# Sixteen more ticks behind the gate columns, the high parts of q on GpSimd, and fewer maxima taken off by VectorE, in a kernel of attention and two expert layers

## The chip, the cores and the metric

One core of one Trainium2 chip. The metric is the device time of one execution in microseconds (us), the median of three runs. Names: PE is TensorE, DVE is VectorE, ACT is ScalarE, POOL is GpSimd, and SP (SyncE) issues most of the loads.

## The reference, cut to what matters

Attention with random features, then a product of four weights, then an expert layer in which each token goes to one expert. Inputs are float32; the weights of the middle part come to the chip as float64 words and are turned into float32 there.

```python
def phi(x):                                   # x is q or k, 2 x 8 heads x 576 tokens x 64
    proj = np.einsum('bhsd,md->bhsm', x, omega)          # 128 features
    h = proj - np.sum(x * x, axis=-1, keepdims=True) / 2.0
    h = h - np.max(h, axis=-1, keepdims=True)
    return np.exp(h) / np.sqrt(m)
q_p, k_p = phi(q_s), phi(k_s)
kv, z = np.einsum('bhsm,bhsd->bhmd', k_p, v), np.sum(k_p, axis=2)
x = np.einsum('bhsm,bhmd->bhsd', q_p, kv) / (np.einsum('bhsm,bhm->bhs', q_p, z)[..., None] + 1e-06)
x = ((x @ w1) * (x @ w2)) @ w3 @ w_out        # 1152 tokens, 512 -> 1024 -> 1024 -> 512
...
expert_idx = np.argmax(x @ w_gate, axis=1)    # 8 experts, capacity 288 tokens
h = np.maximum(np.einsum('ecd,edf->ecf', disp, e1), 0.0)
y = np.einsum('ecf,efd->ecd', h, e2)          # weighted by the gate, scattered back to the tokens
```

## The kernel before, in words

Every large matrix product is done with operands split into a high part (rounded to a TensorE format) and a low part (what rounding left): three matmuls, high by high, low by high, high by low. So each operand needs a copy that rounds and a subtraction, on whichever engine is chosen for it, before PE may use it.

**Attention** (to about 100 us). Tokens come in nine tiles of 128, first of k (k0 to k8), then of q (q0 to q8). `split` (L195) makes the high part with an ACT copy (L198) and the low part with a subtraction on POOL (L199; DVE for k0 and k2). `phi` (L202) does a group of four heads: twelve matmuls (L210), a maximum on DVE (L212), and then one of two ways. With the group in `SUBK` or `SUBQ`, DVE subtracts the maximum (L215) and ACT does one exponential of 512 columns (L216); otherwise ACT does four exponentials of 128 columns with the maximum as bias (L219). `q_tr` (L221) transposes the features of q, which ACT copies out (L227); `num` (L254) and `x_tr` (L272) make x and its two parts.

**Weights.** A chunk of 128x512 float64 words goes through five steps: a load (SP), three bit operations on DVE (L325 to L327, or L350, L351 and L355), a cast to the high part on ACT (L330 or L360), the low part on POOL (L331 or L364). The float32 words `w_f` have two buffers, which the low part on POOL sets free.

**Middle** (to about 250 us). PLAN gives the order of PE's work: `ab` (L425) are the products x@w1 and x@w2 of one block f of 128 columns, whose product g is made by DVE (L448) or, for some, by ACT and POOL (L445, L446); `W` (L465) is w3@w_out of one block, copied out twice by ACT (L478, L479) and its low part made by POOL (L480); `gate_t` (L487) and `gate_u` (L496) make the columns of W times w_gate, with the ACT copies L494 and L501; `logits` use these.

**Order.** PE's order is that of the text throughout. Up to the mark "|" in PLAN a scheduler places the instructions of DVE, ACT, POOL and SP; behind it those engines too keep the order of the text, and each works strictly in its order. Behind the mark, conversions of weights are tasks in a list; `tick()` (L133) hands out the next stage of up to two tasks that hold a raw buffer, one stage per engine and tick. Ticks stand behind each half of `ab`, inside and behind `W` and behind `logits`. `need` ticks until a weight is there.

**Experts** (from about 230 us). END is the order of the last stretch, a letter per step and "." for a tick. `r0` and `r1` are the first expert chunk of each batch half. For each: `to_features` (letters t, T; L812) transposes gathered rows, with ACT L824 and DVE L825; `product` (p, P; L830) multiplies by W, with copies L839 (ACT) and L840 (DVE); `hidden` (h, H; L845) multiplies by e1 and `result_t` (s, S; L885) by e2, with ACT L898, transposes L901, and `scatter` (L868): DVE L870 and an indirect DMA by POOL to `out` (L871). The expert weights have no float64 step: load by SP (L739), high parts of their two halves on ACT (L752), low part of half 0 on DVE and of half 1 on POOL (L756); the low part of half 1 sets the raw buffer free for the next load. The quarters 0 and 2 share one ring of two raw buffers, 1 and 3 another of two. A digit in END lets the tasks of a matrix start: "3" is e1 of r1, "4" is e2 of r1; "x" and "y" hand these tasks in. In the names of the trace the numbers of experts and buffers are left out: `r_e_20h` is the high part of half 0 of quarter 2, of e1 or e2, of either chunk.

Of the kernel before, what the change touches and what calls it, by code (L numbers as in the profile page):

```python
# [33 lines left out]
DVE_LOW = ("k0", "k2")  # L34

SUBK = [(0, 1), (), (0, 1), (0, 1), (), (), (), (), ()]
SUBQ = [(1,), (0, 1), (0, 1), (1,), (), (1,), (1,), (), (1,)]

KV_AT = {2: (0,), 4: (1, 2), 6: (3, 4), 8: (5, 6), 10: (7, 8)}

# [14 lines left out]

END = "l<kAkrArfAAArfw>AAAA>AA<At.ttLttMt>1K.p..K.p..Rp..p..p..RpF.2h..h.R.h..Fh..h..h..x3h..h..s.TT.sTT.sTT.s..ssy4P..P..P..P..P..P..P.H.H.H.H.H.HHHSSSS"


@with_exitstack
def attention_moe_kernel(ctx: ExitStack, tc: tile.TileContext, qT, kT, v, om, w1, w2, w3, wo, wg, e1, e2, cap, out):
    nc = tc.nc
    V = nc.vector
    A = nc.scalar
# [15 lines left out]
    def px(nm):  # L81
        return psx.tile([128, 512], F32, tag="px", name=nm)
# [4 lines left out]
    def kq(shape, dt, nm):  # L87
        return kqp.tile(shape, dt, tag="kq", name=nm)

    def wt(tag, shape, dt, nm):  # L90
        return big.tile(shape, dt, tag=tag, name=nm, bufs=BUFS[tag])
# [20 lines left out]
    late, hold, leave = [False], [False], set()  # L112
# [9 lines left out]
    def pump():  # L122
        full = set()
        for t in todo:
            r = t["ring"]
            if r and t["raw"] is None and r not in full:
                if out_of[r] < LIM[r]:
                    out_of[r] += 1
                    t["raw"] = t["load"]()
                else:  # L130
                    full.add(r)

    def tick(n=1):  # L133
        for _ in range(0 if hold[0] else n):
            used = set()
            while todo and (todo[0]["key"][0][0] != "e" or todo[0]["key"][:2] in leave) and (todo[0]["ring"] is None or sum(t["ring"] is not None for t in active) < 2):
                active.append(todo.pop(0))
            for t in list(active):
                engs, fn, end = t["st"][0]
                if used & set(engs):  # L140
                    continue
                used |= set(engs)
                t["st"].pop(0)
                fn(t)
                if end:
                    out_of[t["ring"]] -= 1
                    pump()
                if not t["st"]:
                    active.remove(t)
                    done_of[t["key"]] = t["got"].get("r", True)  # L150
# [44 lines left out]
    def split(src, i, nm):  # L195
        t = wt("hl", [128, 2, 512], F32R, f"{nm}{i}_hl")
        raw = src[i].rearrange("p k t -> p (k t)")
        A.copy(out=t[:, 0], in_=raw)  # L198
        (V if nm + str(i) in DVE_LOW else nc.gpsimd).tensor_tensor(out=t[:, 1], in0=raw, in1=t[:, 0].bitcast(F32), op=ALU.subtract)  # L199
        return t  # L200

    def phi(dst, t, g, nm, sub):  # L202

        ps = pa(f"pj{nm}_{g}")
        p3 = ps.rearrange("p (h m) -> p h m", m=M)
        mx = sm.tile([128, 4], F32, tag="mx", name="mx", bufs=4)
        for r in range(2):
            k = 2 * g + r
            for n, (s, w) in enumerate(PASS):
                nc.tensor.matmul(out=ps[:, r * 256:(r + 1) * 256], lhsT=t[:, s, k * 128:(k + 1) * 128], rhs=om_hl[:, w],  # L210
                                 start=(n == 0), stop=(n == 2))
        V.tensor_reduce(out=mx, in_=p3, axis=AX, op=ALU.max, negate=True)  # L212
        d3 = dst[:, 4 * g:4 * g + 4, :]
        if g in sub:
            V.tensor_tensor(out=d3, in0=p3, in1=mx.unsqueeze(2).to_broadcast([128, 4, M]), op=ALU.add)  # L215
            A.activation(out=d3, in_=d3, func=ACTF.Exp)  # L216
        else:
            for h in range(4):
                A.activation(out=d3[:, h, :], in_=p3[:, h, :], func=ACTF.Exp, bias=mx[:, h:h + 1])  # L219
# [83 lines left out]
    def split_to(n):  # L303
        while len(hls) < min(n, 18):
            w, i = order[len(hls)]
            load_to(len(hls) + 1 + AHEAD)
            hls[len(hls)] = split(kt if w == "k" else qt, i, w)

    def phi_g(n, g):
# [3 lines left out]
        if g == 0:  # L313
            split_to(n + 1)
            (kp if w == "k" else qp)[i] = wt("ph", [128, H, M], F32, f"{w}p{i}")
        phi((kp if w == "k" else qp)[i], hls[n], g, f"{w}{i}", (SUBK if w == "k" else SUBQ)[i])

# [169 lines left out]
    def gate_t(f):  # L487

        raw = raws.pop(f)
        ps = px(f"wT{f}")  # L490
        for d in range(4):
            nc.tensor.transpose(out=ps[:, d * 128:(d + 1) * 128], in_=raw[:, d * 128:(d + 1) * 128], identity=ident)
        wT[f] = kq([128, 4, 128], F32, f"wT{f}")
        A.copy(out=wT[f], in_=ps.rearrange("p (d m) -> p d m", d=4))  # L494

    def gate_u(f):  # L496
        ps = px(f"u{f}")
        t = wT.pop(f)
        for d in range(4):
            nc.tensor.matmul(out=ps[:, 0:E], lhsT=t[:, d], rhs=wgT[:, d], start=(d == 0), stop=(d == 3))  # L500
        A.copy(out=u_all[:, f], in_=ps[:, 0:E])  # L501

    def logits(f, cs):
        for c in cs:
            nc.tensor.matmul(out=lgp[c * 32:c * 32 + E, 0:C], lhsT=u_all[:, f], rhs=g_t[f][:, c * C:(c + 1) * C],
                             start=(f == 0), stop=(f == 7))
        if late[0]:
            tick()
# [70 lines left out]
    for p in PLAN.split():  # L579
# [10 lines left out]
        elif what == "u":  # L590
            gate_t(*arg)
        elif what == "v":
            gate_u(*arg)
        elif what == "o":
            conv_o(*arg)
        elif what == "t":
            conv3(*arg)
        elif what == "l":
            logits(*arg, range(4))
        elif what == "h":  # L600
            logits(*arg, range(2))
        elif what == "e":
            for w in range(2):
                ab_mm(*arg, w)
        elif what == "z":
            zeroed()
        elif what == "|":
            flush()
            late[0] = True
            mark()  # L610
        elif what == "g":

            wg_sb = kq([E, DM], F32, "wg_sb")
            nc.sync.dma_start(out=wg_sb, in_=wg)
            ps = px("wgT")
            for d in range(4):
                nc.tensor.transpose(out=ps[:, d * E:(d + 1) * E], in_=wg_sb[:, d * 128:(d + 1) * 128], identity=ident[:E, :E])
            A.copy(out=wgT, in_=ps[:, 0:4 * E].rearrange("p (d e) -> p d e", e=E))
# [341 lines left out]

    for p in END:
        if p == "A":
# [119 lines left out]
```

## Time and profile before

| | us |
|---|---|
| three runs | 343.56, 344.31, 346.01 |
| median | 344.31 |
| the profiled execution | 343.41 |
| its span | 341.5 |
| around the span | 1.9 |
| PE busy | 325.2 (95%) |
| DVE busy | 218.8 (64%) |
| ACT busy | 146.4 (43%) |
| POOL busy | 134.2 (39%) |

The span runs from the first to the last instruction that the profile shows. A row of a timeline reads: start, duration, engine, line, operation, what it writes and reads, how many in a row, and in brackets how long the engine had been idle before it and who ended that.

### The profile page before, as it was taken

What the parts mean: (1) busy time and instruction counts of PE and PEld (TensorE: products, weight loads), DVE (VectorE), ACT (ScalarE), POOL (GpSimd) and SP (SyncE); (2) the same over time, 40 slices, a digit from 0 to 9 for tenths busy, and PEclk for the clock granted to TensorE, in tenths of its full rate; (3) what the DMA queues carried; (4) which work ended last, traced back from release to release, by engine and by line L of the source; (5) the groups of instructions that cost most, each with busy time, mean ns of one, the idle gap of its engine ahead of it and who ended that gap; (6) DMA issues with size and microseconds to landing.
All of it is one profiled execution on the core that took longest, in us unless ns stands there. A gap on an engine that the chain in (4) does not pass through costs nothing. (4 is left out here: it accounts for less than half of the span.)

```text
span 341.5 us, 7108 instructions
## 1 busy us (share of the span) xinstructions
PE 325.2 (95%) x2771; PEld 300.8 (88%) x2771; DVE 218.8 (64%) x426; ACT 146.4 (43%) x347; POOL 134.2 (39%) x118
## 2 busy tenths in 40 slices
PE   8999989999999999999998898999999998999991
PEld 6899889999998889898878786899899998999991
DVE  4979999999986864935394763281596766332110
ACT  4999899743321413324333332121462645332100
POOL 3737910333353324545336664014062562243021
PEclk9999999999999999999999999999999999999997
DMA  7995200344465728972335430893869791510011
GB/s 253 396 316 199 64 2 7 97 147 125 126 184 163 270 38 190 211 148 61 125 89 157 134 114 0 289 129 88 298 112 183 224 274 41 209 48 2 1 30 46
DMA packets 25147, 47.76 MB, mean 140 GB/s; under 512 B 3116, under 2 KB 12460, under 8 KB 25110
## 3 DMA queue, kind: packets, MB, share of 16 engines
q1 hardware_dynamic: 16950, 40.18, 39.0%
q10 hardware_dynamic: 7104, 3.54, 6.3%
q0 software_dynamic: 1056, 3.54, 3.8%
q8 instruction: 24, 0.39, 0.5%
q14 instruction: 13, 0.11, 0.1%
HBM read 38.98 MB, written 8.27 MB: 138 GB/s over the span
## 5 line engine op out<-in xcount | busy, mean ns | idle before, releaser
L433 PE MATMUL ab<-xh,w_hl 128*128 128x288 f32 x512 | 108.2, 299 | 4.8 <-POOL w_hl L364 3.8
L433 PEld LDWEIGHTS ab<-xh,w_hl 128*128 128x128 f32 x512 | 83.4, 188 | 8.1 <-POOL w_hl L364 4.5
L433 PE MATMUL ab<-xl,w_hl 128*128 128x288 f32 x256 | 75.5, 295 | 0.0
L433 PEld LDWEIGHTS ab<-xl,w_hl 128*128 128x128 f32 x256 | 48.1, 188 | 0.0
L472 PE MATMUL W<-wo_hl,w_hl 128*128 128x512 f32 x192 | 46.3, 397 | 0.0
L472 PEld LDWEIGHTS W<-wo_hl,w_hl 128*128 128x128 f32 x192 | 35.5, 188 | 8.2 <-issue 0.5
L350 DVE TENSOR_SCALAR w_f<-w_raw 128x512 uint32<-128x512 uint32 x22 | 17.4, 789 | 23.5 <-POOL w_hl L364 23.4
L364 POOL TENSOR_TENSOR w_hl<-w_f,w_hl 128x512 fp32r<-128x512 f32 x22 | 29.6, 1358 | 5.3 <-ACT w_hl L360 5.3
L405 DVE STREAM_TRANSPOSE gs<-g 128x576 f32<-128x576 f32 x16 | 19.5, 1221 | 13.5 <-POOL g L446 13.3
L836 PE MATMUL r_x2p<-r_xc,W 128*128 128x288 f32 x192 | 26.5, 297 | 0.0
L836 PEld LDWEIGHTS r_x2p<-r_xc,W 128*128 128x128 f32 x192 | 25.7, 188 | 0.1
L480 POOL TENSOR_TENSOR W<-W_raw,W 128x512 fp32r<-128x512 f32 x8 | 10.8, 1355 | 37.3 <-ACT W L479 19.2
L331 POOL TENSOR_TENSOR wo_hl<-wo_f,wo_hl 128x512 fp32r<-128x512 f32 x8 | 11.5, 1433 | 34.7 <-PE xT L276 18.4
L437 ACT COPY a_sb<-ab 128x288 f32<-128x288 f32 x32 | 12.7, 398 | 27.6 <-PE ab L433 27.6
L331 POOL TENSOR_TENSOR w_hl<-w_f,w_hl 128x512 fp32r<-128x512 f32 x10 | 14.0, 1402 | 22.4 <-ACT w_hl L330 22.4
L360 ACT CAST w_hl<-w_f 128x512 fp32r<-128x512 f32 x22 | 13.7, 625 | 18.8 <-DVE w_f L355 18.8
L446 POOL TENSOR_TENSOR g<-a_sb,b_sb 128x288 f32<-128x288 f32 x12 | 10.6, 879 | 25.0 <-ACT b_sb L445 25.0
L355 DVE SCALAR_TENSOR_TENSOR w_f<-w_raw,w_f 128x512 uint32<-128x512 uint32 x22 | 19.2, 872 | 0.6
L871 POOL DMA_INDIRECT out<-r_yo,r_odx x6 | 5.6, 932 | 34.4 <-DVE r_yo L870 22.6
L448 DVE TENSOR_TENSOR g<-a_sb,ab 128x288 f32<-128x288 f32 x20 | 8.9, 448 | 15.4 <-PE ab L433 15.4
L210 PE MATMUL pjq<-om_hl,q_hl 128*128 128x256 f32 x108 | 16.3, 293 | 0.0
L210 PE MATMUL pjk<-om_hl,k_hl 128*128 128x256 f32 x108 | 15.6, 297 | 0.6 <-ACT k_hl L198 0.5
(233 smaller groups left out, 693.3 us busy)
## 6 DMA issues: line engine op xcount, KB each, us to landing
w_raw<-in_w SPq DMA_DIRECT2D x32, 512.0 KB, 3.7
wo_raw<-in_wo SPq DMA_DIRECT2D x8, 512.0 KB, 3.5
gd<-gs ACTq DMA_DIRECT2D x12, 288.0 KB, 6.0
v<-in_v SPq DMA_DIRECT2D x9, 260.0 KB
k<-in_kT SPq DMA_DIRECT2D x9, 256.0 KB, 4.3
q<-in_qT SPq DMA_DIRECT2D x9, 256.0 KB, 6.6
out<-zero SPq DMA_DIRECT2D x1, 2304.0 KB, 9.7
r_e_0r<-in_e SPq DMA_DIRECT2D x4, 512.0 KB
```

What stands on the lines that cost most here:

```text
L210: nc.tensor.matmul(out=ps[:, r * 256:(r + 1) * 256], lhsT=t[:, s, k * 128:(k + 1) * 128], rhs=om_hl[:, w], start=(n == 0), stop=(n == 2))
L331: nc.gpsimd.tensor_tensor(out=hl[1], in0=f.bitcast(F32), in1=hl[0].bitcast(F32), op=ALU.subtract)
L350: V.tensor_scalar(out=f, in0=r[:, :, 1], scalar1=3, scalar2=0x3FFFFFF8, op0=ALU.logical_shift_left, op1=ALU.bitwise_and)
L355: V.scalar_tensor_tensor(out=t["f"], in0=r[:, :, 0], scalar=29, in1=t["f"], op0=ALU.logical_shift_right, op1=ALU.bitwise_or)
L360: A.copy(out=h[:, 0], in_=t["f"].bitcast(F32))
L364: nc.gpsimd.tensor_tensor(out=h[1], in0=t["f"].bitcast(F32), in1=h[0].bitcast(F32), op=ALU.subtract)
L405: V.transpose(out=sts[b][:, :, :, f % GF], in_=g_t[f][:, b * S:(b + 1) * S].rearrange("p (j t) -> p j t", t=32))
L433: nc.tensor.matmul(out=p[:, :C], lhsT=w12[f][w][s][:, k, :], rhs=xhl[c][r][:, k], start=(n == 0), stop=(n == 11))
L437: A.copy(out=abp[f, c], in_=p[:, :C])
L472: nc.tensor.matmul(out=p, lhsT=w3_t[f, k // 4][s][:, k % 4, :], rhs=wo_t[k][r], start=(n == 0), stop=(n == 23))
L480: nc.gpsimd.tensor_tensor(out=w_t[f][:, 1], in0=raw, in1=w_t[f][:, 0].bitcast(F32), op=ALU.subtract)
L836: nc.tensor.matmul(out=p4[d][:, :C], lhsT=w_t[f][:, s, d * 128:(d + 1) * 128], rhs=xc[r][f // 4][:, f % 4], start=(f == 0 and (s, r) == (0 ...
```

## The change

Four edits. (1) `SUBQ` keeps four of the nine groups of q whose maximum DVE takes off: q1 group 0, q2 group 0, q5, q6 and q8 group 1 go to the way with four exponentials on ACT. (2) The high part of the nine tiles of q is copied by POOL and no longer by ACT; k stays. (3) `gate_t` and `gate_u` each end with a tick: sixteen in all. (4) In END, "3" moves from right behind "x" to behind the first "TT"; between "3" and "y4" stood ten ticks, and now six.

```diff
-SUBQ = [(1,), (0, 1), (0, 1), (1,), (), (1,), (1,), (), (1,)]
+SUBQ = [(1,), (1,), (1,), (1,), (), (), (), (), ()]
...
-END = "...x3h..h..s.TT.sTT.sTT.s..ssy4P..P.....
+END = "...xh..h..s.TT.3sTT..sTT..s..ssy4P..P.....
...
     def split(src, i, nm):
         t = wt("hl", [128, 2, 512], F32R, f"{nm}{i}_hl")
         raw = src[i].rearrange("p k t -> p (k t)")
-        A.copy(out=t[:, 0], in_=raw)
+        (A.copy if nm == "k" else nc.gpsimd.tensor_copy)(out=t[:, 0], in_=raw)
...
     def gate_t(f):
...
         A.copy(out=wT[f], in_=ps.rearrange("p (d m) -> p d m", d=4))
+        if late[0]:
+            tick()
...
     def gate_u(f):
...
         A.copy(out=u_all[:, f], in_=ps[:, 0:E])
+        if late[0]:
+            tick()
```

Lines from `gate_t` on have numbers two, and from `gate_u` on four higher in the changed kernel.

What moves on POOL in the attention, at the first tiles of q (`w_0_hl` and `w_1_hl` are low parts of w1 and w2, blocks 0 and 1). Before:

```order
L199 TENSOR_TENSOR q_hl<-q_343,q_hl 128x512
L331 TENSOR_TENSOR w_0_hl<-w_0_f,w_0_hl 128x512
L199 TENSOR_TENSOR q_hl<-q_377,q_hl 128x512
L331 TENSOR_TENSOR w_0_hl<-w_0_f,w_0_hl 128x512
L199 TENSOR_TENSOR q_hl<-q_446,q_hl 128x512
L199 TENSOR_TENSOR q_hl<-q_478,q_hl 128x512
L331 TENSOR_TENSOR w_1_hl<-w_1_f,w_1_hl 128x512
```

Of the changed kernel, from the same place:

```order
L198 CAST q_hl<-q_343 128x512
L199 TENSOR_TENSOR q_hl<-q_343,q_hl 128x512
L198 CAST q_hl<-q_377 128x512
L199 TENSOR_TENSOR q_hl<-q_377,q_hl 128x512
L198 CAST q_hl<-q_446 128x512
L199 TENSOR_TENSOR q_hl<-q_446,q_hl 128x512
L198 CAST q_hl<-q_478 128x512
L199 TENSOR_TENSOR q_hl<-q_478,q_hl 128x512
L198 CAST q_hl<-q_580 128x512
L331 TENSOR_TENSOR w_0_hl<-w_0_f,w_0_hl 128x512
```

The first low part of a weight stood behind one row of q and now stands behind nine.

What moves on POOL around block 5 of W (`w_5_hl` are the low parts of w1 and w2 of block 5, in this order; `w_6_0_hl` one of w3; W_2501 and W_2515 are W of block 5). Before:

```order
L364 TENSOR_TENSOR w_5_hl<-w_5_f,w_5_hl 128x512
L480 TENSOR_TENSOR W_2501<-W_raw,W_2501 128x512
L364 TENSOR_TENSOR w_5_hl<-w_5_f,w_5_hl 128x512
L446 TENSOR_TENSOR g_2549<-a_sb,b_sb 128x288
L364 TENSOR_TENSOR w_6_0_hl<-w_6_0_f,w_6_0_hl 128x512
```

Of the changed kernel:

```order
L364 TENSOR_TENSOR w_5_hl<-w_5_f,w_5_hl 128x512 x2
L480 TENSOR_TENSOR W_2515<-W_raw,W_2515 128x512
L364 TENSOR_TENSOR w_6_0_hl<-w_6_0_f,w_6_0_hl 128x512
L446 TENSOR_TENSOR g_2568<-a_sb,b_sb 128x288
```

The low part of w2 passed from behind W's low part to ahead of it; blocks 6 and 7 read alike.

What moves on POOL at the end of r0 (the rows r_e are low parts of e1 of r1, quarters 0 to 3; the one that follows them, again r_e_00l, is of e2 of r1). Before:

```order
L756 TENSOR_TENSOR r_e_00l<-r_e_0r,r_e_00h 128x512
L756 TENSOR_TENSOR r_e_10l<-r_e_1r,r_e_10h 128x512
L756 TENSOR_TENSOR r_e_20l<-r_e_2r,r_e_20h 128x512
L756 TENSOR_TENSOR r_e_30l<-r_e_3r,r_e_30h 128x512
L871 DMA out<-r_yo_3878,r_odx 1152x512
L871 DMA out<-r_yo_3883,r_odx 1152x512
L871 DMA out<-r_yo_3888,r_odx 1152x512
L756 TENSOR_TENSOR r_e_00l<-r_e_0r,r_e_00h 128x512
```

Of the changed kernel:

```order
L760 TENSOR_TENSOR r_e_00l<-r_e_0r,r_e_00h 128x512
L760 TENSOR_TENSOR r_e_10l<-r_e_1r,r_e_10h 128x512
L875 DMA out<-r_yo_3881,r_odx 1152x512
L875 DMA out<-r_yo_3886,r_odx 1152x512
L875 DMA out<-r_yo_3891,r_odx 1152x512
L760 TENSOR_TENSOR r_e_20l<-r_e_2r,r_e_20h 128x512
L760 TENSOR_TENSOR r_e_30l<-r_e_3r,r_e_30h 128x512
L760 TENSOR_TENSOR r_e_00l<-r_e_0r,r_e_00h 128x512
```

The low parts of quarters 2 and 3 of e1 of r1 passed from ahead of the three scatters to behind them. ACT's order at the product of r1 is the same in both: two casts of quarter 2 of e2, the copy L839 of the product's third part, two casts of quarter 3, the fourth copy.

## Rows read from the trace of the kernel before

**Rows 1.** The page's first part: busy time, share, instructions

```profile
PE 325.2 (95%) x2771; PEld 300.8 (88%) x2771; DVE 218.8 (64%) x426; ACT 146.4 (43%) x347; POOL 134.2 (39%) x118
```

**Rows 2.** Windows: stretch, length, busy of PE, PEld, DVE, ACT, POOL; clock, DMA, GB/s

```profile
20.00:40.00 20.00, 19.89 (x328) 18.61 (x330) 18.66 (x29) 18.58 (x56) 12.34 (x9) 1.00 0.49 163
40.00:60.00 20.00, 18.62 (x268) 17.32 (x264) 18.91 (x56) 18.11 (x51) 4.38 (x4) 1.00 0.12 31
```

**Rows 3.** Waits of PE: who, for whom, us in total, times, longest

```profile
PE ab L433 <- POOL w_hl L364: 3.8, 3, 1.5
PE tq L226 <- ACT qpT L227: 1.4, 1, 1.4
...
PE r_pt L820 <- DVE r_xc L825: 0.9, 1, 0.9
```

**Rows 4.** PE's timeline behind W of block 5

```profile
181.74 0.53 PE L433 MATMUL ab<-xh,w_hl 128*128 128x288 f32 x2 [1.02 <-POOL w_hl L364]
```

**Rows 5.** POOL's timeline of the same stretch

```profile
174.20 1.29 POOL L364 TENSOR_TENSOR w_hl<-w_f,w_hl 128x512 fp32r<-128x512 f32 x1 [1.28 <-ACT w_hl L360]
179.17 1.29 POOL L480 TENSOR_TENSOR W<-W_raw,W 128x512 fp32r<-128x512 f32 x1 [3.68 <-ACT u_all L501]
180.42 1.26 POOL L364 TENSOR_TENSOR w_hl<-w_f,w_hl 128x512 fp32r<-128x512 f32 x1
```

**Rows 6.** ACT's timeline of the same stretch

```profile
177.26 0.62 ACT L360 CAST w_hl<-w_f 128x512 fp32r<-128x512 f32 x1 [3.14 <-DVE w_f L355]
```

**Rows 7.** Groups of instructions by form: busy us, mean ns of one, idle before

```profile
L199 POOL TENSOR_TENSOR q_hl<-q,q_hl 128x512 fp32r<-128x512 f32 x9 | 12.7, 1428 | 0.0
...
L219 ACT ACTIVATE qp<-pjq,mx 128x128 f32<-128x128 f32 x36 | 10.4, 409 | 0.0
...
L215 DVE TENSOR_TENSOR qp<-pjq,mx 128x512 f32<-128x512 f32 x9 | 6.1, 685 | 0.0
L198 ACT CAST q_hl<-q 128x512 fp32r<-128x512 f32 x9 | 6.1, 750 | 0.0
L216 ACT ACTIVATE qp<-qp 128x512 f32<-128x512 f32 x9 | 5.7, 645 | 0.2 <-DVE qp L215 0.2
...
L571 POOL MEMSET zero<- 128x512 f32 x1 | 0.5, 518 | 0.0
```

**Rows 8.** DVE's timeline in the attention: the same bit operation twice

```profile
21.66 0.42 DVE L325 TENSOR_SCALAR w_f<-w_raw 128x512 uint32<-128x512 uint32 x1
...
34.82 1.33 DVE L325 TENSOR_SCALAR w_f<-w_raw 128x512 uint32<-128x512 uint32 x1
```

**Rows 9.** POOL's timeline at the scatters of r0

```profile
293.80 0.97 POOL L871 DMA_INDIRECT out<-r_yo,r_odx  x1 [2.29 <-DVE r_yo L870]
300.67 0.95 POOL L871 DMA_INDIRECT out<-r_yo,r_odx  x1 [5.91 <-DVE r_e_20l L756]
304.22 0.92 POOL L871 DMA_INDIRECT out<-r_yo,r_odx  x1 [2.60 <-DVE r_x2l L840]
305.16 1.31 POOL L756 TENSOR_TENSOR r_e_00l<-r_e_0r,r_e_00h 128x512 fp32r<-128x512 f32 x1
```

**Rows 10.** PE's timeline: product of r1, and its hidden layer's first matmul

```profile
292.64 13.02 PE L836 MATMUL r_x2p<-r_xc,W 128*128 128x288 f32 x96
305.51 0.30 PE L857 MATMUL r_hp<-r_x2h,r_e_00h 128*128 128x288 f32 x1
```

**Rows 11.** ACT's timeline: third copy of the product of r1

```profile
303.31 0.40 ACT L839 CAST r_x2h<-r_x2p 128x288 fp32r<-128x288 f32 x1 [0.96 <-PE r_x2p L836]
```

**Rows 12.** SP's timeline: issue of the load of e2's quarter 2

```profile
290.89 0.33 SPq L739 DMA_DIRECT2D r_e_2r<-in_e  x1
```

**Rows 13.** DMA issues: count, KB, median us to landing

```profile
r_e_1r<-in_e SPq DMA_DIRECT2D x4, 512.0 KB, 3.6
```

**Rows 14.** Windows at the end: the clock is the column behind POOL

```profile
334.00:335.00 1.00, 0.54 (x4) 0.18 (x2) 0.42 (x1) 0.00 (x0) 0.00 (x0) 1.00 0.00 0
...
337.00:338.00 1.00, 0.00 (x0) 0.00 (x0) 0.00 (x0) 0.00 (x0) 0.00 (x0) 0.79 0.71 197
```

More of the change, by code (lines that the diff above doesn't have):

```diff
@@ L53 @@
 )
-END = "l<kAkrArfAAArfw>AAAA>AA<At.ttLttMt>1K.p..K.p..Rp..p..p..RpF.2h..h.R.h..Fh..h..h..x3h..h..s.TT.sTT.sTT.s..ssy4P..P..P..P..P..P..P.H.H.H.H.H.HHHSSSS"
+END = "l<kAkrArfAAArfw>AAAA>AA<At.ttLttMt>1K.p..K.p..Rp..p..p..RpF.2h..h.R.h..Fh..h..h..xh..h..s.TT.3sTT..sTT..s..ssy4P..P..P..P..P..P..P.H.H.H.H.H.HHHSSSS"
 @with_exitstack
```

## The prediction

> **What bounds the kernel now.** First the page's first part: PE is busy for 325.2 of 341.5 us, 95% [rows 1], so the kernel is bound by PE wherever nothing makes PE wait, and no edit takes a matmul away. What can be won is what PE waits for, what can be lost is a new wait. So the waits of PE come next [rows 3]: three times, 3.8 us in all, it waits for a weight's low part from POOL; once for 1.4 us, in the attention, for a copy by ACT; once for 0.9 us for the low part of gathered rows near the end. Then, for each of these, the timelines of the engine that is waited for. The windows show who has room in the attention: from 20 to 60 us DVE and ACT are busy for over 18 of each 20 us, POOL for 12.34 of the first 20 and 4.38 of the second [rows 2].
>
> **The added ticks (edit 3).** They issue no new instruction: they hand out stages of conversions sooner. The wait at 181.74 us is that for w2 of block 5 [rows 4]. Its cast was done at 177.26 + 0.62 = 177.88 us [rows 6]. But POOL's next instruction in order was W's low part, which waited for ACT's copies until 179.17, and only behind it, at 180.42, came the low part that PE wanted [rows 5]. It could have run from 177.88 to 179.1, 2.5 us sooner than it ended (180.42 + 1.26 = 181.7). In the new order it stands ahead of W's low part; the other two waits are of the same kind, for blocks 6 and 7, and the longest of the three is 1.5 us [rows 3], all under 2.5. W's low part comes 1.3 us later in exchange, and nothing reads it before the experts, so that costs nothing. What is late next would be the step ahead, the cast and DVE's words; the ticks bring these forward too. Bounds: 0 (another stage is late in its place) and -3.8; I take **-3.8**, since the order removes the very cause that the rows show.
>
> **The attention (edits 1 and 2).** ACT loses nine copies, 6.1 us in all; five groups go from one exponential of 5.7 / 9 = 0.63 us to four of 10.4 / 36 = 0.29 us, which adds 5 x (1.16 - 0.63) = 2.6. ACT: -3.5 us. DVE loses five subtractions of 0.685: -3.4 us. POOL gains nine copies of 128x512 [rows 7]. No row shows such a copy. From below it is bounded by POOL's fill of the same tile, which reads nothing, 0.52 us, from above by its subtraction, which reads two tiles, 1.43 us; it reads one, so I take the middle, 1.0, that is 9.0 us (4.7 to 12.9). POOL has 20 - 12.34 = 7.7 us free from 20 to 40 us [rows 2], where most of these copies fall: 1.3 us too much. What stands behind is the low parts of the first weights (the order shows the first of them behind nine rows of q where it stood behind one). These set the two word buffers free, so DVE, working in order, waits for them with the maxima of q behind: +1.3 at most for PE. The second cost is on DVE: its bit operation takes 0.42 us alone and 1.33 beside POOL's subtractions [rows 8], 0.9 more. POOL has no pauses left, so more of them meet: I count three more, 2.7 us. DVE's relief of 3.4 covers most of it: 1.3 + 2.7 - 3.4 = **+0.6**. PE's wait of 1.4 us hangs on the same chain (ACT's copy behind a cast that waits for DVE's words), so I let it stay. Bounds: copies of 0.52 fit into the gaps, and the 1.4 goes, -1.5 with what ACT gains; copies of 1.43 are 12.9 - 7.7 = 5.2 too many, and with the relief some +4.
>
> The rows show 0.42 against 1.33 us for the same operation [rows 8]. The Trainium skill, "SBUF — State Buffer", section "Who interferes with whom", says that DVE and GpSimd share a pair of ports that one instruction holds to its end while the other stands still. It speaks against this edit, and the row agrees: by it every one of the nine copies could hold up one operation of DVE, the second rival below, where my sum has three. The page "GPSIMD Engine Reference", section 3.1, has 769 ns for 512 elements in a loop with one input; no row here shows it. Nine of these would be an estimated 6.9 us, which fits into POOL's gaps, and the sum would lose its 1.3.
>
> **The end (edit 4).** Fewer casts of expert weights now stand on ACT ahead of the copies of gathered rows, so PE's wait of 0.9 us [rows 3] should go: -0.9. But the low parts of quarters 2 and 3 of e1 of r1 now stand behind POOL's three scatters. Let T be the start of the product of r1 (292.64) [rows 10]. The scatters started at T + 1.2, T + 8.0 and T + 11.6 [rows 9]; the second and third are put down to DVE instructions whose results they don't use, so I read these gaps as the wait until the scatter before has landed, all three writing the same output. In before the load of quarter 2 of e2 was issued at 290.89, ahead of T [rows 12]. Now its buffer comes free only behind a low part that follows the third scatter. The gaps were 6.9 and 3.6 us; three loads ran beside the first, of which two now come later, so I take 4.5 and 3.6: third scatter T + 9.3 to 10.2, the low parts (1.3 each [rows 9]) until 11.5 and 12.8, load issued at 11.6, landed 3.6 later [rows 13] at T + 15.2. ACT's order is unchanged: two casts of that quarter (0.62, as [rows 6], some 1.1 together) come ahead of the third copy of the product (0.40 [rows 11]), whose low part on DVE follows with about as much: ready at T + 17.2. PE ends the product at T + 12.9 [rows 10] and can do 12 more matmuls of 12.87 / 96 = 0.134 us without that part, until T + 14.5: it waits 2.7 us. The fourth part, behind quarter 3's casts, comes 1.3 + 0.3 later, 0.8 of it beyond PE's next six matmuls: 3.5 in all. With -0.9 that is **+2.6**. Bounds: with the gaps as they were (6.9), +5.0; if the scatters don't wait, -0.9.
>
> **Sum.** -3.8 + 0.6 + 2.6 = -0.6 on the profiled execution, which took 343.41 us (span 341.5 and 1.9 around it): 342.8. The median of the runs shown, 344.31, lies 0.9 higher: **343.7 us**. Within 1%, 3.4 us, a measurement of this kernel can hardly tell a change from none; this is within.
>
> **Rivals.**
> First, *the scatters don't wait for each other*. Then POOL issues them at T + 1.2 to 4, the low parts are done by T + 7, the loads land by T + 11, and PE never waits: 343.41 - 3.8 + 0.6 - 0.9 = 339.3, as a median 340.2; with the attention at its better bound 338.1. For it: the rows name DVE and no transfer as what ended the gaps [rows 9]. Against: the gaps are there, 5.91 and 2.60 us, and a scatter uses nothing of what these DVE instructions make.
>
> Second, the other side: *POOL's copies hold DVE in the attention*, all nine and not three. Nine times 0.9 is 8.2 us on DVE; with the 1.3 and less the 3.4 that is +6.1: 343.41 - 3.8 + 6.1 + 2.6 = 348.3, as a median 349.2. It decides from about five operations so held on, where DVE's relief is used up (5 x 0.9 = 4.5 against 3.4), DVE being over 93% busy there [rows 2]. Against: POOL's low parts already run beside DVE for 12 of 20 us, and PE is still 19.89 of 20 busy.
>
> Third, *the ticks move nothing that PE sees*: DVE's words are late instead. 343.41 + 0.6 + 2.6 = 346.6, as a median 347.5. Against: the cast lay ready for 2.5 us.
>
> A further cost is left outside the cases: PE's clock falls after a long pause. At the end it was still at its upper level (1.00, 2.4 GHz) when PE stopped at about 334.5 us and fell to the lower (1.2 GHz) at about 337.6 (0.79 as the mean of that microsecond) [rows 14], 3 us later. [...]
>
> **How the numbers follow.** Forecast 0.48; first rival 0.25; second 0.19; third 0.08. Faster by over 1% (under 340.9) come 0.20 of the first rival and 0.06 of the forecast's lower edge (both terms at their good ends); slower by over 1% (over 347.8) 0.16 of the second, 0.04 of the third and 0.06 of the forecast with the long gap. That is 0.26, 0.48 and 0.26. The range goes from 339.5, within the first rival, to 349.0, within the second; the forecast's own is 341 to 347.5 (tail from +1.7 to +5.0, attention from -1.5 to +2).
>
> **What would show it.** Right: no wait of PE's x products for POOL's low parts; three scatters of r0 in a row with gaps of 3 to 5 us, loads of e2's quarters 2 and 3 issued about 11 us behind the start of r1's product, and PE waiting 2 to 4 us for the third part's low half. In the attention POOL without gaps from 20 to 45 us, the copy at about 1 us, PE's idle time about as before. Wrong: hidden of r1 starting without a wait (first rival); copies over 1.3 us, with PE waiting for maxima or exponentials (second); 3 to 4 us of waits left at blocks 5 to 7 (third).

## The result and the profile after

The changed kernel took 348.05 us in the median of four runs (347.24 to 349.04), the kernel before 344.12: a ratio of 1.0108 with a 95% interval of 1.0076 to 1.0141. It is slower by 1.1%, where the forecast was no change (343.7): inside the whole range (339.5 to 349.0), and above the forecast's own (341 to 347.5). The profiled execution took 347.24 us, 3.8 more than that of before.

The page's first part of the changed kernel, which answers to [rows 1], and its waits of PE, which answer to [rows 3]:

```profile
PE 325.7 (94%) x2771; PEld 300.9 (87%) x2771; DVE 216.8 (63%) x421; ACT 144.7 (42%) x353; POOL 143.0 (41%) x127
```

```profile
PE pjq L210 <- ACT qp L219: 2.6, 1, 2.6
PE r_hp L861 <- ACT r_x2h L843: 1.8, 1, 1.8
...
PE ab L433 <- ACT a_sb L437: 1.1, 1, 1.1
PE nu L262 <- ACT a_sb L437: 1.0, 1, 1.0
PE tq L226 <- ACT qp L216: 0.9, 1, 0.9
PE nu L262 <- DVE x L269: 0.6, 2, 0.3
```

PE is busy as long as before (325.7 against 325.2 us). The three waits for POOL's low parts are gone, as forecast, and so is the one for gathered rows. New are a wait of 2.6 us at the first groups of q, several small ones in the rest of the attention, and one of 1.8 behind r1's product.

The order of PE's work is the same in all kernels here, so the same matmuls can serve as milestones. The table gives, from the PE timeline of each profiled run, how many us longer each stretch took than in before; the single edits and the later runs are explained in the next section. The milestones are the starts of: the first matmul of a q group (29.47 us in before), the first transposes of q's features (35.37), those of w_gate (83.70), the first W (110.83), r0's gather indices (229.75), r1's product (292.64), the last matmul of r1's hidden layer (318.16); and PE's end (334.54).

| kernel | to q | to q's transposes | to w_gate | to W | to gather | to r1's product | to end of hidden | sum at PE's end |
|---|---|---|---|---|---|---|---|---|
| changed | +0.5 | +2.7 | +2.8 | +0.3 | -4.8 | -1.2 | +3.6 | +3.8 |
| ticks_only | +0.1 | 0.0 | 0.0 | -0.1 | -4.7 | +2.3 | 0.0 | -2.4 |
| end_only | +0.3 | 0.0 | 0.0 | +0.2 | 0.0 | -1.1 | +3.5 | +3.0 |
| copies_only | +0.3 | +2.8 | -0.4 | +0.5 | 0.0 | +2.2 | 0.0 | +5.4 |
| subq_only | +1.1 | 0.0 | +3.2 | -0.5 | 0.0 | -0.4 | 0.0 | +3.6 |
| subq_early | +0.6 | 0.0 | -0.5 | +2.9 | 0.0 | +0.4 | 0.0 | +3.3 |
| subq_late | +0.5 | 0.0 | +1.5 | -1.1 | 0.0 | 0.0 | 0.0 | +1.0 |
| subq_c2first | -0.2 | 0.0 | +0.5 | +0.7 | 0.0 | 0.0 | 0.0 | +0.9 |
| fill_copy | 0.0 | +2.0 | +3.2 | +0.3 | -4.8 | -1.0 | +3.5 | +3.3 |
| fill_low | +0.4 | +1.0 | +2.9 | +0.2 | -4.8 | -1.0 | +5.3 | +4.1 |
| ticks_end2 | +0.1 | 0.0 | 0.0 | +0.3 | -4.7 | -1.2 | +3.7 | -1.8 |
| ticks_end3 | +1.5 | 0.0 | -0.1 | 0.0 | -4.7 | -1.2 | 0.0 | -4.5 |
| end3_late_copies | +0.4 | 0.0 | -0.7 | +0.2 | -4.7 | -1.2 | 0.0 | -6.1 |

For the changed kernel the last three stretches (to gather, to r1's product, to the end of hidden) come out nearly as forecast; the attention does not: 2.7 + 2.8 + 0.3 = 5.8 us, where the sum had 0.6.

The place of the first 2.7 us is DVE's timeline. First before, then the changed kernel: the last four of nine bit operations ahead of the first maximum of q, and that maximum:

```profile
28.48 0.69 DVE L327 SCALAR_TENSOR_TENSOR w_f<-w_raw,w_f 128x512 uint32<-128x512 uint32 x1
29.09 0.42 DVE L325 TENSOR_SCALAR w_f<-w_raw 128x512 uint32<-128x512 uint32 x1
29.55 0.69 DVE L326 SCALAR_TENSOR_TENSOR w_f<-w_raw,w_f 128x512 uint32<-128x512 uint32 x1
30.27 0.69 DVE L327 SCALAR_TENSOR_TENSOR w_f<-w_raw,w_f 128x512 uint32<-128x512 uint32 x1
30.88 0.68 DVE L212 TENSOR_REDUCE mx<-pjq 128x4 f32<-128x512 f32 x1
```

```profile
30.07 1.66 DVE L327 SCALAR_TENSOR_TENSOR w_f<-w_raw,w_f 128x512 uint32<-128x512 uint32 x1
31.65 0.83 DVE L325 TENSOR_SCALAR w_f<-w_raw 128x512 uint32<-128x512 uint32 x1
32.51 1.65 DVE L326 SCALAR_TENSOR_TENSOR w_f<-w_raw,w_f 128x512 uint32<-128x512 uint32 x1
34.20 1.65 DVE L327 SCALAR_TENSOR_TENSOR w_f<-w_raw,w_f 128x512 uint32<-128x512 uint32 x1
35.77 0.68 DVE L212 TENSOR_REDUCE mx<-pjq 128x4 f32<-128x512 f32 x1
```

The maximum comes 4.9 us later, and DVE waits for nobody from 22 us to it: its nine bit operations take 11.3 us in place of 6.0. POOL's timeline shows what ran beside them. In before it has two pauses, 5.87 us up to 25.20 and 2.46 us up to 30.36, and seven of the nine operations start in these, at their short times of 0.42 and 0.69:

```profile
25.20 1.29 POOL L331 TENSOR_TENSOR w_hl<-w_f,w_hl 128x512 fp32r<-128x512 f32 x1 [5.87 <-ACT w_hl L330]
26.45 1.46 POOL L199 TENSOR_TENSOR q_hl<-q,q_hl 128x512 fp32r<-128x512 f32 x1
30.36 1.76 POOL L331 TENSOR_TENSOR w_hl<-w_f,w_hl 128x512 fp32r<-128x512 f32 x1 [2.46 <-ACT w_hl L330]
```

In the changed kernel it has no pause there, and the copy itself is cheap, 0.60 us where DVE is quiet and 1.07 where it is not:

```profile
18.74 0.60 POOL L198 CAST q_hl<-q 128x512 fp32r<-128x512 f32 x1
...
31.12 1.07 POOL L198 CAST q_hl<-q 128x512 fp32r<-128x512 f32 x1
32.28 1.34 POOL L199 TENSOR_TENSOR q_hl<-q,q_hl 128x512 fp32r<-128x512 f32 x1
33.58 1.72 POOL L331 TENSOR_TENSOR w_hl<-w_f,w_hl 128x512 fp32r<-128x512 f32 x1
```

### The profile page after: what moved, and what is told of

Its sections match the earlier page's. It is cut to its first block, busy times and chain, and to the rows that moved or that the text cites. A ratio compares the mean times of both kernels' runs of the same rounds, so it can differ in the third digit from the quotient of the medians.

```text
span 345.5 us, 7114 instructions
## 1 busy us (share of the span) xinstructions
PE 325.7 (94%) x2771; PEld 300.9 (87%) x2771; DVE 216.8 (63%) x421; ACT 144.7 (42%) x353; POOL 143.0 (41%) x127
## 5 line engine op out<-in xcount | busy, mean ns | idle before, releaser
L350 DVE TENSOR_SCALAR w_f<-w_raw 128x512 uint32<-128x512 uint32 x22 | 15.5, 705 | 16.4 <-POOL w_hl L364 15.6
L355 DVE SCALAR_TENSOR_TENSOR w_f<-w_raw,w_f 128x512 uint32<-128x512 uint32 x22 | 21.2, 964 | 0.7
L446 POOL TENSOR_TENSOR g<-a_sb,b_sb 128x288 f32<-128x288 f32 x12 | 12.0, 1002 | 20.0 <-ACT b_sb L445 20.0
L219 ACT ACTIVATE qp<-pjq,mx 128x128 f32<-128x128 f32 x56 | 16.6, 399 | 2.5 <-DVE mx L212 2.4
```

What stands on the lines that cost most here:

```text
L350: V.tensor_scalar(out=f, in0=r[:, :, 1], scalar1=3, scalar2=0x3FFFFFF8, op0=ALU.logical_shift_left, op1=ALU.bitwise_and)
L355: V.scalar_tensor_tensor(out=t["f"], in0=r[:, :, 0], scalar=29, in1=t["f"], op0=ALU.logical_shift_right, op1=ALU.bitwise_or)
```

## The experiments

### The four edits one at a time

Each is the kernel before with one edit: the sixteen ticks (ticks_only), the new END (end_only), the copies on POOL (copies_only), the new SUBQ (subq_only).

> The kernel before with the sixteen ticks alone. Theory A (the change's loss lies in the attention, in the copies of q on GpSimd; the ticks gain what the late waits held): the three waits of TensorE's x products for GpSimd's low parts go, the attention stays as before: 4 to 5 us less than before, some 339.5. Rival B (the loss comes from the ticks too, since the ready conversions push the other work on VectorE and ScalarE back): the waits go but come back elsewhere behind 110 us, 342 or more.

Measured: 340.99, ratio 0.9884 (0.9821 to 0.9947). The late waits are gone and 4.7 us with them, before r0's gather; nothing came back in the middle part, so B falls. But 2.3 us are lost near the end. PE's timeline there, and the windows around it:

```profile
279.01 1.33 PE L824 MATMUL r_pt<-ident,r_xg 96*128 96x96 f32 x8 [1.75 <-DVE r_xc L829]
```

```profile
275.00:280.00 5.00, 3.25 (x26) 2.99 (x25) 2.17 (x5) 2.42 (x6) 0.68 (x1) 0.98 0.43 146
280.00:285.00 5.00, 5.00 (x29) 5.00 (x29) 2.13 (x4) 1.30 (x4) 0.60 (x1) 0.68 0.00 0
```

The wait for gathered rows, 0.9 us in before, is 1.75, and behind it TensorE's granted clock (the column behind POOL) is 0.98 and 0.68 as means of 5 us: it was at its lower level (1.2 GHz) for (0.02 + 0.32) / 0.5 x 5 = 3.4 us. With PE busy throughout that is an estimated loss of half, 1.7 us. One of the four runs took 338.93; whether the clock stayed up in it is not shown.

> The kernel before with the new order of the end alone. Theory A: the wait of 0.9 us for gathered rows goes, and TensorE waits some 3 to 3.6 us behind r1's product for the casts of e2's quarters 2 and 3, whose loads come behind the three scatters: 2.4 us slower than before, some 346.5. Rival C (the scatters are only slow where the late waits of the middle part are gone): within 1 us of before.

Measured: 347.72, ratio 1.0103 (1.0079 to 1.0127); in the profile 1.1 us gained and 3.5 lost, as A says. C falls. The profiled run (346.35) is the lowest of ten; the median lies 3.6 us above before, more than A's 2.4, and what raised it is not shown.

> The kernel before with the high parts of q on GpSimd alone. Theory A (GpSimd's copies hold VectorE's two-operand bit operations, the first maxima of q come 4 to 5 us late, and conversions come late from then on): 5 to 7 us slower, 349 to 351, VectorE's L326 and L327 between 22 and 36 us at 1.6 us in place of 0.7. Rival D (the four exponentials per group on ScalarE make the loss, the copies are harmless): within 1.5 us of before.

Measured: 346.65, ratio 1.0069 (1.0039 to 1.0099). The first maximum is late as in the changed kernel and the loss of 2.8 us is in the same stretch; D falls for this half. The median is under A's 349 to 351. The profiled run (348.76) is the second highest of ten, and in it the clock was lowered twice. The first time is behind the wait for exponentials, 2.8 us here; by then the wait of 1.4 us of [rows 3] is gone, but the clock takes back most of that gain:

```profile
35.00:40.00 5.00, 2.34 (x15) 2.16 (x16) 5.00 (x11) 3.39 (x9) 4.66 (x6) 0.91 0.37 107
40.00:45.00 5.00, 5.00 (x55) 4.86 (x55) 5.00 (x8) 3.93 (x9) 4.50 (x4) 0.75 0.27 52
```

The second time (0.83 from 285 to 290 and from 290 to 295 us) is behind a wait of 1.53 us for gathered rows; with it the +2.2 ahead of r1's product belongs to the clock and that wait, and not to the attention.

> The kernel before with the five groups of q moved from VectorE's subtraction to four exponentials on ScalarE alone. Theory A: VectorE gains 3.4 us, ScalarE loses 2.6, and the time stays within 1 us of before. Rival D: ScalarE, over 18 of 20 us busy from 20 to 60 us, makes the features of q late, and the time grows by 4 to 6 us.

Measured: 347.69, ratio 1.0102 (1.0045 to 1.0159). A falls here: the moved groups cost by themselves, 3.2 us between q's first transposes and w_gate's. D's 4 to 6 us are not reached, and its cause is not shown by this run. So the loss in the attention has two parts, one for each edit. The four edits do not simply add: their medians lie -3.1, +3.6, +2.5 and +3.6 us from before, 6.6 together, and the whole change 3.9. In the profiles the 2.3 and 2.2 us that ticks_only and copies_only lose ahead of r1's product are not there with the new END.

### What makes the copies dear: fill_copy and fill_low

fill_copy, in the changed kernel:

```diff
-        (A.copy if nm == "k" else nc.gpsimd.tensor_copy)(out=t[:, 0], in_=raw)
+        A.copy(out=t[:, 0], in_=raw) if nm == "k" else nc.gpsimd.memset(t[:, 0].bitcast(F32), 0.0)
```

> The changed kernel with each of GpSimd's nine copies of q's high part replaced by a fill with zeros of the same tile, which reads nothing; the high part of q is so left out of the features. VectorE's and ScalarE's orders are those of the changed kernel row for row. Theory A1 (a copy holds VectorE's two-operand operations because both read SBUF through what they share): the fills hold nobody, L326 and L327 in the attention fall back towards 0.7 us beside them, the first maximum of q comes 2 to 4 us sooner and the kernel is 2 to 3 us faster than the changed one, 345 to 346. Rival A2 (it is GpSimd's subtractions alone that hold VectorE; the copies cost by filling GpSimd): the fills save 9 times 0.3 us of GpSimd's time, VectorE's operations stay at 1.6, and the kernel gains under 1 us.

Measured: 347.59; 0.5 us under the changed kernel, as A2 says. DVE's nine operations take 10.7 us in place of 11.3, so it is not mainly the copies that hold them, and A1 falls. The copies have a smaller part: the stretch to q's transposes costs 2.0 in place of 2.7.

```profile
30.16 1.81 DVE L327 SCALAR_TENSOR_TENSOR w_f<-w_raw,w_f 128x512 uint32<-128x512 uint32 x1
...
33.07 1.65 DVE L327 SCALAR_TENSOR_TENSOR w_f<-w_raw,w_f 128x512 uint32<-128x512 uint32 x1
34.64 0.68 DVE L212 TENSOR_REDUCE mx<-pjq 128x4 f32<-128x512 f32 x1
```

fill_low, in the changed kernel (for q alone):

```diff
-        ... nc.gpsimd.tensor_tensor(out=t[:, 1], in0=raw, in1=t[:, 0].bitcast(F32), op=ALU.subtract)
+        [nc.gpsimd.memset(t[:, 1].bitcast(F32), 0.0) for _ in range(3)]
```

> The changed kernel with GpSimd's nine subtractions for q's low part replaced by three fills with zeros each, 3 x 0.52 = 1.56 us for 1.56 us, so GpSimd has as much to do but reads nothing there; the low part of q is so left out of the features. VectorE's and ScalarE's orders stay. Theory A2 (GpSimd's two-operand subtractions, which now run without a pause beside VectorE's first bit operations, hold these): L326 and L327 between 22 and 36 us fall from 1.65 to 0.7, the first maximum of q comes 3 to 4 us sooner, TensorE's wait of 2.6 us goes, 2.5 to 3.5 us less than the changed kernel: 345. Rival I (VectorE is late because GpSimd is full and the words wait for low parts): the operations may be short, but the time stays within 1 us of the changed kernel's 348.

Measured: 347.21. The stretch to q's transposes costs 1.0 us in place of 2.7, and the wait of 2.6 us for exponentials is gone (0.9 for the copies themselves is there). DVE's timeline:

```profile
30.87 1.76 DVE L325 TENSOR_SCALAR w_f<-w_raw 128x512 uint32<-128x512 uint32 x1
32.66 0.69 DVE L326 SCALAR_TENSOR_TENSOR w_f<-w_raw,w_f 128x512 uint32<-128x512 uint32 x1
33.39 0.69 DVE L327 SCALAR_TENSOR_TENSOR w_f<-w_raw,w_f 128x512 uint32<-128x512 uint32 x1
34.00 0.68 DVE L212 TENSOR_REDUCE mx<-pjq 128x4 f32<-128x512 f32 x1
```

Beside fills the two-operand L326 and L327 are at 0.69 again; the six of them take 5.8 us together, in before 4.6 and in the changed kernel 9.4. The one-operand L325 is now the one that is held (1.76); whether by the fills or by the copies beside it is not separated. So the nine take 9.7 us, still 3.7 over before, and by PE's milestone POOL's subtractions make some two thirds of this part (1.7 of 2.7). That is what the Trainium skill, "SBUF — State Buffer", section "Who interferes with whom", says: a DVE operation with two SBUF inputs meets a GpSimd operation that reads, not one that only writes, and tensor_scalar can take the shared pair too. The time itself moved by 0.8 us, less than A2 said and as little as rival I did, so A2 rests on the profile: in it 1.7 us were ahead at r0's gather, and then the same wait at the end as in the changed kernel was followed by the lower clock (0.66 from 310 to 315 us), +5.3 in place of +3.6.

### What makes the moved groups dear

subq_early moves q1 and q2 alone, subq_late q5, q6 and q8.

```diff
+SUBQ = [(1,), (1,), (1,), (1,), (), (1,), (1,), (), (1,)]          # subq_early
+SUBQ = [(1,), (0, 1), (0, 1), (1,), (), (), (), (), ()]            # subq_late
```

> The kernel before with q1 group 0 and q2 group 0 alone moved from VectorE's subtraction to four exponentials on ScalarE. Theory E (the loss of 3.6 us in the moved groups comes from ScalarE being full while the last q tiles pass, from 50 to 66 us, where three of the five groups lie; casts of weights stand behind their exponentials, so low parts, words and x come late): within 1 us of before. Rival F (any such move costs, by the 0.5 us that ScalarE spends more per group): two fifths of it, 1.4 us slower, 345.5.

> The kernel before with q5, q6 and q8 group 1 alone moved to four exponentials on ScalarE. Theory E: nearly all of the loss, 3 to 3.6 us slower, 347 to 348, with TensorE falling behind between 58 and 78 us. Rival F: three fifths, 2.1 us slower.

Measured: 345.38, ratio 1.0017 (0.999 to 1.0044), and 344.44, ratio 1.0008 (0.999 to 1.0025). The first fits E, and F's 1.4 us at the edge of its interval; the second fits neither E nor F. The profile of subq_late loses 1.5 us where E looked for 3, that of subq_early 2.9 at another place, in a wait of 2.2 for ACT's a_sb behind a cast of w_out that passed ahead of it, with the clock low behind it. Two moves that cost little apart cost 3.6 together, so neither ScalarE's load in the late groups nor a price per group explains it; what is left to test is the order that the scheduler makes of the whole. In subq_only ACT's casts of w1 and w2 of block 2 stand ahead of that of wo7, whose words DVE makes first; in before wo7 comes first on every engine. DVE's timeline of subq_only shows what follows:

```profile
59.32 0.43 DVE L325 TENSOR_SCALAR w_f<-w_raw 128x512 uint32<-128x512 uint32 x1 [1.59 <-POOL w_hl L331]
...
65.58 0.43 DVE L325 TENSOR_SCALAR wo_f<-wo_raw 128x512 uint32<-128x512 uint32 x1 [0.38 <-POOL w_hl L331]
...
70.66 1.49 DVE L325 TENSOR_SCALAR wo_f<-wo_raw 128x512 uint32<-128x512 uint32 x1 [0.79 <-POOL wo_hl L331]
```

Three waits for a word buffer with maxima and x behind them; before has none there, the changed kernel the same three (1.15, 0.38, 0.79). To test this, subq_c2first is subq_only with

```diff
-    "g o7 a01 c2 o4 a10 ...
+    "g c2 a01 o7 o4 a10 ...
```

> The five moved groups alone, as in subq_only, but with the conversions of w1 and w2 of block 2 ahead of that of the first part of w_out (o7) in PLAN, so that words, casts and low parts of these three weights come in one order on VectorE, ScalarE and GpSimd. Theory H (in subq_only the words of o7 are made first, but its cast comes last; they hold one of the two word buffers for 20 us, VectorE waits for low parts with maxima and x behind it, and TensorE falls back by 3.3 us between 58 and 78 us): VectorE's waits go and the kernel is within 1.5 us of before, 345.5 at most. Rival E (it is ScalarE's load alone): 347 to 348, as in subq_only.

Measured: 345.48, ratio 1.0038 (1.0002 to 1.0074). In its profile (344.04 us) the stretch costs 0.5 in place of 3.2, and the three waits are gone. H stands, and E falls. The profiled run is the lowest of ten (344.04 to 348.44); what raised the others is not shown. Nor was this order tried in the changed kernel itself: that its 2.8 us in this stretch have the same cause rests on the same three waits.

### The end, and a better kernel

ticks_end2 and ticks_end3 are ticks_only with another END:

```diff
-...x3h..h..s.TT.sTT.sTT.s..ssy4P...        # before
+...xh..h..s.TT.3sTT..sTT..s..s....sy4P...  # ticks_end2
+...xh..h..s.TT.3s..TT..sTT...s..ssy4P...   # ticks_end3
```

> The kernel before with the sixteen ticks, with the start of e1 of r1 behind the first pair of steps as in the change, but with four more ticks between the last transposes of r0 and its scatters, so that the low parts of quarters 2 and 3 stand ahead of the scatters again; the attention as before. Theory A: 4.8 us from the late waits and 0.9 to 1.7 from the rows' wait at the end, and no wait behind r1's product: 6 us faster than before, some 338. Rival G (the low parts now delay the scatters, and the casts of e2 still come late): a wait of 1 us or more for the casts of e2 remains, 340 or more.

Measured: 341.23, ratio 0.9891 (0.9847 to 0.9935). The low parts are ahead of the scatters and the casts of e2 are on time; but on DVE low parts that wait for ACT's late casts now stand ahead of the rows that free PE's accumulators:

```profile
PE r_x2p L840 <- DVE r_yo L874: 1.9, 1, 1.9
```

A wait for a wait, and again the lower clock behind it (0.66 from 290 to 295 us): +3.7. Rival G was right that one stays, though at another place.

> The kernel before with the sixteen ticks and an order of the end in which e1 of r1 starts behind the first pair of steps, as in the change, but all its casts except one half stand ahead of the last copy of r0's result, so that neither the scatters nor VectorE's scaled rows wait for them. Theory A: no wait for gathered rows, none of 1.9 us at the start of r1's product as in ticks_end2, none behind it: 337.5 to 339. Rival G (one of the three waits stays, and the clock falls behind it): 340 or more.

Measured: 338.62 (338.25 to 338.68), ratio 0.9816 (0.9765 to 0.9867). No wait is left at either place, and the four runs agree within 0.5 us. The profile's +1.5 ahead of q comes with a wait of 1.79 us at 10.1 us for a copy of k and a clock of 0.66 from 10 to 15 us.

end3_late_copies adds the copies on POOL for four tiles:

```diff
-        A.copy(out=t[:, 0], in_=raw)
+        (A.copy if nm == "k" or i < 5 else nc.gpsimd.tensor_copy)(out=t[:, 0], in_=raw)
```

> ticks_end3 with the high parts of q5 to q8 alone on GpSimd; those of q0 to q4 stay on ScalarE, and so stays GpSimd's order up to the low part of w1 of block 1; VectorE's order is that of before throughout. Theory J (the copies cost by where they stand: those of the first q tiles let GpSimd's subtractions run without pauses beside VectorE's first bit operations; the late ones harm nobody and take the queue off ScalarE that makes TensorE wait 1.4 us for the first transposed features): VectorE's words between 21 and 31 us as in before, no loss at the first q group, the wait of 1.4 us shorter or gone, 337 to 338.7. Rival K (GpSimd's copies cost wherever they stand, in proportion, four ninths of some 3 us): 340.

Measured: 337.72 (337.37 to 338.4), ratio 0.981 (0.9778 to 0.9841), faster than both kernels. J stands: DVE's words are as in before,

```profile
29.48 0.42 DVE L325 TENSOR_SCALAR w_f<-w_raw 128x512 uint32<-128x512 uint32 x1
29.94 0.69 DVE L326 SCALAR_TENSOR_TENSOR w_f<-w_raw,w_f 128x512 uint32<-128x512 uint32 x1
30.66 0.69 DVE L327 SCALAR_TENSOR_TENSOR w_f<-w_raw,w_f 128x512 uint32<-128x512 uint32 x1
31.27 0.68 DVE L212 TENSOR_REDUCE mx<-pjq 128x4 f32<-128x512 f32 x1
```

and the wait of 1.4 us is 0.6. Whether its gain over ticks_end3 is more than the difference of two separate comparisons is not settled by the medians (0.9 us apart); the stretch from q's transposes to w_gate, -0.7 against -0.1, speaks for it.

## Why the prediction was wrong

**The ticks: right.** Forecast -3.8, measured -4.7 to -4.8. The three waits give back 4.25 us of it, 0.15 each more than their idle time (1.17 for 1.02): the matmuls here start 0.13 us apart and last 0.29, and across a wait they do not overlap. POOL's timeline shows the step as it was put: both low parts ahead of W's.

```profile
179.16 2.54 POOL L364 TENSOR_TENSOR w_hl<-w_f,w_hl 128x512 fp32r<-128x512 f32 x2
185.34 1.29 POOL L480 TENSOR_TENSOR W<-W_raw,W 128x512 fp32r<-128x512 f32 x1 [3.65 <-ACT W L479]
```

**The end: right, in place and size.** Forecast +2.6, measured -1.2 + 3.6 = +2.4. With T the start of r1's product (292.89), POOL, SP, ACT and PE of the changed kernel:

```profile
294.73 0.97 POOL L875 DMA_INDIRECT out<-r_yo,r_odx  x1 [2.93 <-DVE r_yo L874]
298.75 0.95 POOL L875 DMA_INDIRECT out<-r_yo,r_odx  x1 [3.05 <-DMA out<-r_yo,r_odx]
302.30 0.92 POOL L875 DMA_INDIRECT out<-r_yo,r_odx  x1 [2.61 <-ACT r_x2h L843]
303.24 1.31 POOL L760 TENSOR_TENSOR r_e_20l<-r_e_2r,r_e_20h 128x512 fp32r<-128x512 f32 x1
```

```profile
304.57 0.33 SPq L743 DMA_DIRECT2D r_e_2r<-in_e  x1
```

```profile
308.22 0.62 ACT L756 CAST r_e_20h<-r_e_2r 128x512 fp32r<-128x512 f32 x1 [6.23 <-SPq L1007]
```

```profile
309.71 0.40 PE L861 MATMUL r_hp<-r_x2h,r_e_00h 128*128 128x288 f32 x1 [1.76 <-ACT r_x2h L843]
```

The third scatter starts at T + 9.4 (forecast 9.3), the load is issued at T + 11.7 (11.6) and its cast runs at T + 15.3 (15.2). PE's first matmul with the third part's low half follows at 310.20, T + 17.3 (17.2); the 1.76 us are only the idle time up to the high half, and shorter waits follow. The second scatter's releaser is now named as the transfer to `out`, which speaks against the first rival: the scatters wait for each other. One thing of the end was not in the sum: ticks_only loses 2.3 us at the gathered rows, and the new END takes that away with the 0.9.

**The attention: wrong, and it decides.** Forecast +0.6, measured +5.8. Two steps failed. First, "I count three more": eight of the nine bit operations between 22 and 36 us grew, together from 6.0 to 11.3 us. The sum compared POOL's busy share of 20 us with DVE's and did not look where POOL's pauses lay: just beside these operations. The second rival counted all nine (8.2 us), at a chance of 0.19, and put it on the copies; the runs put most of it on POOL's subtractions, which no longer wait for ACT and so leave DVE no pause. Half of its sign came: PE waits for exponentials, with copies of 0.60 to 1.07 us and not over 1.3. The overfull POOL, the other term (+1.3), did not show: in copies_only DVE never waits for POOL in the attention. The price of a copy, 1.0, was near enough.

Second, the five moved groups were costed by their engine time, 2.6 us more on ACT and 3.4 less on DVE, and the relief of 3.4 was taken off the sum. Their order was not read beyond POOL's first rows: the scheduler placed two conversions ahead of a third whose words are made first, and DVE waited for a buffer. That is the stretch of 2.8 us of the 5.8, by the same three waits as in subq_only, and no rival had it. That the second rival's time, 349.2, lies near the measured 348.05 is therefore in part luck: its +6.1 stood for one cause, and the 5.8 us have two.

**The clock.** The forecast left it outside its cases, and shows it falling 3 us after PE's end. In other runs here it fell behind single waits of 1.5 to 2.8 us (last section). The profile of the changed kernel shows it at its upper level behind its waits of 2.6 and 1.8 us, so the 3.8 us between the two profiled runs are not the clock's.

## What to carry to other kernels

An operation moved to another engine lets what waited for its result run earlier and closer together: look where the pauses lie that this fills, count what the earlier work then meets there, and not only the time of the operation. Where a scheduler places the work, read its whole new order on the engines around an edit: the same weights must come in the same order on every engine that hands them on, or one of them sits on a buffer. And put an instruction that waits for a transfer where nothing that PE needs soon stands behind it, on each of the engines that hand the data on.

## What was not expected of the hardware

TensorE's granted clock dropped to its lower level behind single waits of PE, for 3.4 us each time, and not behind each. It was lowered behind waits of 1.75 us (ticks_only), 2.8 and 1.5 (copies_only), 2.2 (subq_early), 1.9 (ticks_end2), 1.95 (fill_low) and 1.8 (ticks_end3), and stayed at 1.00 behind 2.6 and 1.8 in the profiled run of the changed kernel, 2.0 in that of fill_copy and 1.7 in that of end_only. What it costs is seen at r1's hidden layer: the stretch is 5.3 us longer in fill_low, with a wait of 1.95 us and the lower clock, and 3.6 in the changed kernel, with one of 1.76 and the upper.

The changed kernel's four runs took 347.24 and 347.41 us at a mean clock of 0.993 and 0.992, and 348.69 and 349.04 at 0.983 and 0.984. Part of such a difference can lie behind PE's end, where the mean still counts, and ticks_end3's four runs agree within 0.5 us at mean clocks from 0.988 to 0.997. So that the clock made the two higher runs is likely, and not shown.
